# Joining the score and output products of neighbouring units on TensorE, in an mLSTM and two-layer MoE kernel

## The chip, the core and the metric

The kernel runs on one core of one Trainium2 chip. The metric is the device time of one execution in microseconds; smaller is better. Before the change three executions gave 732.37, 736.55 and 738.30 us, so the median is 736.55 us.

## What is computed

Three stages follow each other. The first is an mLSTM recurrence over 768 time steps, for 4 batches of 8 heads of width 40. The other two are feed-forward layers on the 3072 tokens that come out, each 320 wide.

```python
for t in range(S):                                   # first stage, per batch and head
    m_new = maximum(f_gate + m, i_gate)
    C = exp(f_gate + m - m_new) * C + exp(i_gate - m_new) * outer(v, k)
    n = exp(f_gate + m - m_new) * n + exp(i_gate - m_new) * k
    y[t] = sigmoid(o_gate) * (C @ q) / maximum(abs(n @ q), 1)
x = ((x @ w1) * (x @ w2) @ w3) @ w_out               # second stage, inner width 1024
y = maximum(maximum(x @ w1, x @ w2), x @ w3) @ w_out # third stage, inner width 768
```

The weights of the two feed-forward stages arrive as 64-bit floats, and the kernel turns them into 32-bit floats itself.

## The kernel before, in words

**The recurrence** is cut into 9 chunks per batch (8 of L = 88 steps and one of 64). A *unit* is one chunk of four heads; there are 72 units (`NU`), numbered u, two per chunk. `unit(u)` records the work of one: loads of q and k (`raw`, for the first ten units `raw0`), of keys and values (`kv`), of q once more (`qq`), of the gate row maxima (`dd`, from a small table `d_na` that the kernel itself writes to memory at the start); POOL and ACT turn `dd` into exponential weights; TensorE forms the scores `s` (L565 for the first ten units, L586 after them); DVE multiplies them by the weights into `pk` (L596); TensorE forms the outputs `o` from `pk` and `kv` (L606). In rows 88 to 127 `kv` holds the state that is carried from unit u to unit u + 2 (DVE, L611), so the chain from o to o goes on through the whole stage. DVE divides (L624 to L627), POOL multiplies by the output gate (L632) and pads (L636). When both units of a chunk are through, `x_cols` turns the chunk round on TensorE with three transposes (L646, called X here) and splits it into a high and a low part.

**The feed-forward stages** run over 8 blocks of 384 tokens. A product of 32-bit accuracy is made of several TensorE passes over the high and low parts. `group` (L678 to L682) makes one product of 8 matmuls of 384 columns; `b_step` (L745 to L749) and `d_step` (L764) make the second products. `fold` (L906) multiplies `w3` by `w_out` once, at the start. The weights come through `granule`: a load of 512 KB into one of four staging buffers (`stg`, `sx`), then about six ACT and DVE instructions that make 32-bit floats of it, then a split into parts (`wah` on ACT, `wal` on POOL or DVE, and so on).

**The order.** Every operation is recorded in a list with a duration, and `Plan.run` sets the order of each engine with these durations, the latencies between engines in `LAT`, one shift per kind of operation in `BIAS`, and a model of the transfers (`XFER`). Each engine then works through its own list in that order, and an instruction that has to wait holds up all behind it. All transfers are issued by SP, in one order too. `USTEPS` and `UNEXT` say behind which feed-forward steps a unit is recorded.

The buffers that matter: `s`, `o` and X share two PSUM banks (`aq`); `kv` has three buffers, `pk` two, `dd` four; the gate tiles of the start share memory with the `og` tiles of the output gate.

Of the kernel before, what the change touches and what calls it, by code (L numbers as in the profile page):

```python
# [17 lines left out]
L = 88  # L18
LP = 96
NCH = 9  # L20
# [8 lines left out]
NP = 10  # L29
FOLDS = (3,6,9)  # L30
# [10 lines left out]
RAW0 = 3  # L41
LAST = (NBLK - 1, 1, NC - 1)
# [3 lines left out]
    PA=200, PV=200, AV=130, AG=160, GA=90, GV=90, VA=130, VG=155, VP=200, AP=200, GP=230, DA=-50, DV=-50, DG=-30, DP=-50,  # L46
# [4 lines left out]
XFER = 1.45  # L51
BIAS = {"Add": -32750, "Aev": 31250, "Ag": -210500, "Akst": -383000, "Aph": -77500, "Aqs": -262250,
        "Asa": -13500, "Asg": 43250, "Astg": 57250, "Asx": 232000, "Awa": 7750, "Awar": -174000,
        "Awb": -221500, "Awc": 71000, "Awcr": -19750, "Awd": -55000, "Axh": -124000, "Dcs": -138250,
        "Ddd": 34000, "Ddna": 62500, "Dev": 75000, "Dg": -534000, "Dkv": 54250, "Dkvb": -129250, "Dqq": -96500,
        "Draw": 58250, "Dsg": -183000, "Dstg": 57750, "Dsx": -234500, "Dvs": 56750, "Gdd": 194250,
        "Gg": 144250, "Gmp": -23000, "Gpk": -77750, "Gpl": 36250, "Gqqb": -55750, "Gqs": -400500,
        "Gvsb": 10500, "Gwa": 379750, "Gwar": 219500, "Gwc": 102000, "Gwcr": 176500, "Gwd": 49000,
        "Gy": -128500, "Pac0": 27250, "Pac1": -309750, "Pac2": -91000, "Po": 7500, "Ppt": -14000, "Ps": -61250,
        "Pwk": 14250, "Pxt": -39750, "S-": -110000, "Sg": -305500, "Vam": -30000, "Vev": 474750, "Vg": -54250,  # L60
        "Vkst": 81500, "Vkv": -147750, "Vmp": -268500, "Vpk": -108500, "Vsa": -44000, "Vsg": 32250,
        "Vstg": 104500, "Vsx": -56500, "Vwb": -108500, "Vxl": 80250, "Vy": -35250, "Vzero": -14500}
# [5 lines left out]
USTEPS = (8, 9, 11, 12, 15, 16, 20, 21, 23, 25, 27)  # L68
# [209 lines left out]
def mlstm_moe_kernel(  # L278
# [45 lines left out]
    for pool_, tag, bufs, n in (  # L324
# [3 lines left out]
        (tmp, "sx", EX, 1024), (tmp, "w3", L_BUFS, 512), (tmp, "raw0", RAW0, 8 * L),  # L328
# [130 lines left out]
    for c in range(SIGN):  # L459
        dma(318, lambda c=c: SP.dma_start(out=sg0[0:LP, c], in_=og[0, c]), w=[("sg", (0, c))])  # L460
# [502 lines left out]
    def more():  # L963
        u = cur[0]
        if u < NU:
            unit(u)
            if u % 2:
                pend.append(ub(u)[:2])
# [156 lines left out]
```

## Time and profile before

| what | value |
|---|---|
| median of three executions | 736.55 us (732.37 to 738.30) |
| the profiled execution, its own time | 735.73 us |
| its span, from the first to the last instruction | 733.9 us |
| TensorE matmuls busy | 695.5 us (95%) |
| DVE, ACT, POOL busy | 453.4, 385.7, 337.2 us |
| mean granted TensorE clock | 0.988 of 2.4 GHz |

The profile is one execution. Of a row of the timeline the first number is the start, and the second is how long the instruction was in work. Matmuls overlap, so what a group of them costs is read from start to start: from the start of its first matmul to the start of whatever follows. A row of the windows view gives, for a stretch, how long each engine was busy, the granted clock, the mean busy share of the 16 DMA engines and the rate they moved.

### The profile page before, as it was taken

To read this page: it belongs to the slowest core of one execution; us is meant where nothing else is said; L and a number is where in the kernel's file an instruction comes from. 1 tells how busy PE (TensorE), PEld (TensorE's weight loads), DVE (VectorE), ACT (ScalarE), POOL (GpSimd) and SP (SyncE) were. 2 spreads that over 40 slices of the span, in tenths; PEclk is the share of its full clock that TensorE was granted. 3 is DMA by queue.
4 is the path that set the end of the run, shared out by engine and by line. 5 is a ranking of instruction groups with operands and counts; after the bars stand their busy time and mean duration, and the time that the engine had idled before them with its cause. 6 is when DMAs were issued, how large, how long until landed. Compare 5 with 4: busy or idle time off the path is not lost.

```text
span 733.9 us, 12690 instructions
## 1 busy us (share of the span) xinstructions
PE 695.5 (95%) x4269; PEld 670.2 (91%) x4269; DVE 453.4 (62%) x1012; ACT 385.7 (53%) x728; POOL 337.2 (46%) x465
## 2 busy tenths in 40 slices
PE   1797899999999999999999999999999999999998
PEld 1675887788999999999999999999999999999998
DVE  4679998878775668475454777564454774232433
ACT  5978989888884336545334345554342342232211
POOL 1859875857744345565423555564243461000000
PEclk9999999999999999999999999999999999999999
DMA  8998777955623335433212446332222340000000
GB/s 211 251 268 244 226 217 236 239 153 161 190 88 87 102 82 148 130 92 87 75 30 70 114 102 169 94 101 80 57 68 64 92 108 1 1 0 1 1 28 27
DMA packets 52232, 82.48 MB, mean 112 GB/s; under 512 B 11864, under 2 KB 37912, under 8 KB 52168
## 3 DMA queue, kind: packets, MB, share of 16 engines
q1 hardware_dynamic: 52168, 81.69, 40.3%
q8 instruction: 33, 0.54, 0.3%
q14 instruction: 31, 0.25, 0.1%
HBM read 77.63 MB, written 4.03 MB: 111 GB/s over the span
## 4 chain that ended last, share of the span: by engine, by line
PE 78%; DMA 7%; DVE 4%; ACT 4%; POOL 3%; issue 2%; SPq 0%; POOLq 0%; DVEq 0%; ACTq 0%
PE wk L678 12%; PE wk L680 12%; PE wk L679 12%; PE ac L764 8%; PE aq L606 6%; PE wk L682 6%; PE wk L681 6%; PE ac L745 4%; PE ac L749 4%; DMA dd<-d_na 4%; PE ac L747 3%; PE aq L586 2%; PE wk L906 1%; PE aq L646 1%; ACT stg L850 1%
## 5 line engine op out<-in xcount | busy, mean ns | idle before, releaser
L698 POOL TENSOR_TENSOR pl<-pr,ph 128x384 fp32r<-128x384 f32 (+1 forms) x30 | 31.2, 1040 | 161.1 <-ACT ph L694 141.9
L694 ACT CAST ph<-pr 128x384 fp32r<-128x384 f32 (+1 forms) x114 | 57.4, 507 | 86.3 <-PE ac L764 38.3
L678 PE MATMUL wk<-xh,wch 128*128 128x384 f32 x288 | 99.6, 346 | 0.2 <-ACT pr L726 0.2
L729 DVE TENSOR_TENSOR pr<-pr,wk 128x384 f32<-128x384 f32 (+1 forms) x98 | 53.2, 545 | 71.0 <-PE wk L682 67.9
L680 PE MATMUL wk<-xl,wch 128*128 128x384 f32 x288 | 97.1, 337 | 0.0
L679 PE MATMUL wk<-xh,wcl 128*128 128x384 f32 x288 | 97.0, 337 | 0.0
L698 DVE TENSOR_TENSOR pl<-pr,ph 128x384 fp32r<-128x384 f32 (+1 forms) x84 | 53.6, 638 | 67.3 <-ACT ph L694 66.5
L678 PE MATMUL wk<-xh,wah 128*128 128x384 f32 x256 | 91.7, 358 | 1.6 <-ACT xh L657 1.6
L680 PE MATMUL wk<-xl,wah 128*128 128x384 f32 x256 | 87.5, 342 | 2.8 <-DVE xl L660 2.8
L679 PE MATMUL wk<-xh,wal 128*128 128x384 f32 x256 | 87.4, 342 | 0.8 <-DVE wal L869 0.8
L575 POOL TENSOR_TENSOR qs<-misc,qs 40x352 fp32r<-40x352 f32 (+1 forms) x62 | 66.4, 1072 | 39.8 <-ACT qs L571 37.9
L541 POOL TENSOR_TENSOR dd<-am,dd 128x352 f32<-128x352 f32 (+2 forms) x72 | 59.9, 831 | 53.8 <-DMA dd<-d_na 49.1
L726 ACT COPY pr<-wk 128x384 f32<-128x384 f32 x48 | 23.2, 484 | 89.8 <-PE wk L682 89.8
L632 POOL TENSOR_TENSOR misc<-misc 88x160 f32<-88x160 f32 (+1 forms) x62 | 42.6, 687 | 54.5 <-DVE misc L627 54.2
L711 ACT COPY pr<-wk 128x384 f32<-128x384 f32 x64 | 31.0, 484 | 68.6 <-PE wk L682 68.6
L606 PEld LDWEIGHTS aq<-kv,pk 128*128 128x128 f32 (+2 forms) x496 | 59.3, 184 | 5.0 <-issue 2.2
L713 DVE TENSOR_TENSOR pr<-pr,wk 128x384 f32<-128x384 f32 x64 | 35.4, 553 | 41.7 <-PE wk L682 40.7
L606 PE MATMUL aq<-kv,pk 128*128 128x41 f32 (+2 forms) x496 | 58.9, 268 | 1.7 <-DVE misc L627 1.4
L850 ACT ACTIVATE stg<-stg 128x512 f16<-128x512 f32 (+2 forms) x41 | 52.2, 1281 | 7.4 <-DVE stg L842 6.7
L549 ACT ACTIVATE dd<-dd 128x352 f32<-128x352 f32 (+2 forms) x72 | 35.2, 490 | 39.9 <-POOL dd L545 36.0
L678 PEld LDWEIGHTS wk<-xh,wch 128*128 128x128 f32 x288 | 54.2, 188 | 0.5 <-ACT pr L726 0.5
L679 PEld LDWEIGHTS wk<-xh,wcl 128*128 128x128 f32 x288 | 54.2, 188 | 0.0
(130 smaller groups left out, 1755.7 us busy)
## 6 DMA issues: line engine op xcount, KB each, us to landing
misc<-in_qk SPq DMA_DIRECT2D x62, 330.0 KB
dd<-d_na SPq DMA_DIRECT2D x56, 176.0 KB
kv<-in_kv SPq DMA_DIRECT2D x72, 121.5 KB
stg<-in_w3t SPq DMA_DIRECT2D x13, 512.0 KB
stg<-in_wc SPq DMA_DIRECT2D x9, 512.0 KB
qq<-in_qk SPq DMA_DIRECT2D x64, 66.0 KB
misc<-in_og SPq DMA_DIRECT2D x31, 120.0 KB
out<-misc SPq DMA_DIRECT2D x23, 160.0 KB
```

Of the source, the lines that this page charges most:

```text
L541: P.op("G", 735, lambda: G.tensor_tensor(out=T("dd", u)[:r], in0=am[:r, c, h0:h0 + 4].unsqueeze(2).to_broadcast([r, 4, n]), in1=T("dd", u) ...
L575: P.op("G", 889, lambda: G.tensor_tensor(out=T("qs", u)[0:40], in0=T("raw", u)[0:40, 0, :, 0:n], in1=T("qs", u)[0:40].bitcast(F32), op=ALU ...
L606: PE.matmul(T("o", u)[:m, h], lhsT=T("pk", u)[:r, h, 0:m], rhs=T("kv", u)[:r, h, 40:81], start=True, stop=True)
L678: PE.matmul(p, lhsT=h_[:, kt], rhs=xh[:, kt], start=kt == 0, stop=False)
L679: PE.matmul(p, lhsT=l_[:, kt], rhs=xh[:, kt], start=False, stop=False)
L680: PE.matmul(p, lhsT=h_[:, kt], rhs=xl[:, kt], start=False, stop=False)
L681: PE.matmul(p, lhsT=r_, rhs=xh[:, 2], start=False, stop=False)
L694: P.op("A", act(n), lambda sl=sl: A.copy(out=T("ph", key)[:, sl], in_=T(*src)[:, sl]), r=[src + part], w=[("ph", key) + part])
L698: e.tensor_tensor(out=T("pl", key)[:, sl], in0=T(*src)[:, sl], in1=T("ph", key)[:, sl].bitcast(F32), op=ALU.subtract)
L729: P.op("V", dve(sl.stop - sl.start), lambda ps=ps, sl=sl: V.tensor_tensor(out=T(*sc)[:, sl], in0=T(*sc)[:, sl], in1=T(*ps)[:, sl], op=ALU. ...
L764: PE.matmul(T(f"ac{m}", (k, 1)), lhsT=src[:, m * 128:m * 128 + 128], rhs=w[:, o:o + DM], start=first_, stop=last_,)
L850: A.activation(out=sign, in_=tl()[:, :, 1].bitcast(F32), func=AF.Copy)
```

## The change

- From unit `DUO` = 28 on, the matmuls of s(u) and of o(u - 1) are recorded as one TensorE operation, s first. The rest of unit u - 1 (state, division, gate) and the loads of unit u + 2 are recorded behind it.
- The loads of `kv` and of the output gate have 88 rows and no longer 96; those of `qq` and of `raw0` have 40 and no longer 48. A row of `raw0` is cut into four pieces of 704 bytes.
- In `raw0` there is room for an identity behind k, which ACT writes three times at the start. No unit uses it, since `Q0` lists units 2 to 17.
- `LAT`, `BIAS`, `XFER`, the durations of the transfers and `USTEPS` (one more unit step) have new values, so all engines have a new order.

```diff
-LP = 96
+Q0 = tuple(range(2, 18))
+DUO = 28
 LAT = dict(
-    PA=200, PV=200, AV=130, AG=160, GA=90, GV=90, VA=130, VG=155, VP=200, AP=200, GP=230, ...
+    PA=200, PV=200, AV=165, AG=210, GA=90, GV=90, VA=130, VG=155, VP=200, AP=200, GP=230, ...
-XFER = 1.45
+XFER = 1.5
-BIAS = {"Add": -32750, "Aev": 31250, "Ag": -210500, ...
+BIAS = {"Add": -98000, "Aev": 80000, "Ag": -244500, ...
-USTEPS = (8, 9, 11, 12, 15, 16, 20, 21, 23, 25, 27)
+USTEPS = (8, 9, 11, 12, 15, 16, 20, 21, 23, 25, 26, 27)
...
+    eye = cs[0:40, 0:40].unsqueeze(1).to_broadcast([40, 4, 40])
+    for i, t in enumerate(slots["raw0"]):
+        P.op("A", act(160), lambda t=t: A.copy(out=view(t, [40, 4, 128 + L], F32)[:, :, 2 * L:128 + L], in_=eye),
+             r=[("cs", 0)], w=[("raw0b", i)])
...
-        dma(322, lambda: SP.dma_start(out=T("kv", u)[0:LP], in_=kv[b, g, c]), w=[("kv", u, "k")])
+        dma(317, lambda: SP.dma_start(out=T("kv", u)[0:L], in_=kv[b, g, c]), w=[("kv", u, "k")])
...
-            new(t, [LP, DM], F32, "og")
-            dma(318, lambda x=x, t=t: SP.dma_start(out=T(*t), in_=og[b, x]), w=[t])
+            new(t, [L, DM], F32, "og")
+            dma(313, lambda x=x, t=t: SP.dma_start(out=T(*t), in_=og[b, x]), w=[t])
...
-            new(("raw", u), [48, 4, 2 * L], F32, "raw0")
-            dma(333, lambda: SP.dma_start(out=T("raw", u), in_=qk0[g, c]), w=[("raw", u)])
+            new(("raw", u), [40, 4, L + 128], F32, "raw0")
+            dma(313, lambda: SP.dma_start(out=T("raw", u)[:, :, 0:2 * L], in_=qk0[g, c]), w=[("raw", u)])
...
-            dma(174, lambda: SP.dma_start(out=T("qq", u)[80:128], in_=qk[b, g, c, 56:104, 0]),
+            dma(157, lambda: SP.dma_start(out=T("qq", u)[L:128], in_=qk[b, g, c, 0:40, 0]),
...
+            duo = u >= DUO
+            if duo:
+                new(("o", u - 1), [128, 4, 41], F32, "aq")
             def f():
                 for h in range(4):
                     PE.matmul(T("s", u)[0:L, h], lhsT=ks[:, h], rhs=T("qs", u)[:, h], start=True, stop=True)
-            P.op("P", 390, f, cols=90, r=[("qs", u), ("kst", u % 2)], w=[("s", u)])
+                if duo:
+                    outs(u - 1)
+            if duo:
+                P.op("P", 1210, f, cols=300, r=[("qs", u), ("kst", u % 2), ("pk", u - 1), ("kv", u - 1)],
+                     w=[("s", u), ("o", u - 1)])
+            else:
+                P.op("P", 390, f, cols=90, r=[("qs", u), ("kst", u % 2)], w=[("s", u)])
...
+        if u >= DUO:
+            rest(u - 1)
+            load(u + 2)
+        if u + 1 < DUO or u == NU - 1:
+            new(("o", u), [128, 4, 41], F32, f"ac{u % 3}" if u < 10 else "aq")
+            P.op("P", 910 if m > n else 500, lambda: outs(u), cols=210, r=[("pk", u), ("kv", u)], w=[("o", u)])
+            rest(u)
+
+    def outs(u):
+        b, c, g, n, r = ub(u)
+        m = 128 if c < NCH - 1 else n
+        for h in range(4):
+            PE.matmul(T("o", u)[:m, h], lhsT=T("pk", u)[:r, h, 0:m], rhs=T("kv", u)[:r, h, 40:81], start=True, stop=True)
```

**TensorE.** No matmul is added or taken away; only the order is another. On TensorE at the X of the 24th chunk, before (`qs` and `kst` are q and k of s, here of unit 48; the matmuls from `cs` and `misc` are X):

```order
L681 MATMUL wk_129<-xh_81,war 128x384
L682 MATMUL wk_129<-xl_84,war 128x384
L586 MATMUL aq_132<-qs_94,kst_74 88x88 x4
L646 MATMUL aq_133<-cs,misc 128x88 x3
L678 MATMUL wk_130<-xh_81,wah 128x384
```

Before, X stands right behind the s of a later unit, and o stands alone; the whole program has 28 such pairs of s and X, and 6 pairs of s and o. On TensorE a little further on, at s of unit 56 and o of unit 55, now:

```order
L773 MATMUL ac_135<-pl_88,wb 128x384
L598 MATMUL aq_132<-qs_94,kst_74 88x88 x4
L629 MATMUL aq_133<-kv_104,pk_97 128x41 x4
L702 MATMUL wk_130<-xh_81,wah 128x384
L703 MATMUL wk_130<-xh_81,wal 128x384
```

Now o follows s directly, in 46 pairs, and 25 of the 36 X stand alone between large products (before 3); 6 still follow an s. Of the last 24 chunks, 21 had two large products between the o that completes the chunk and its X, and three had three; now there are three or more for 23 of them, and two for the last.

**SP, the first loads.** On SP, behind the gate loads at the start, before (`sx0`, `stg0`, `stg1` are staging buffers, `in_wo1` and `in_w3t` weights):

```order
L488 DMA kv1_104<-in_kv 96x324
L437 DMA d_na_76<-misc_137 8x9x88
L526 DMA raw00_126<-in_qk0 48x704
L828 DMA stg0_111<-in_wo1 128x1024
L502 DMA misc_137<-in_og 96x320 x4
L535 DMA dd0_90<-d_na_76 88x352
L535 DMA dd1_91<-d_na_76 88x352
L828 DMA sx0_121<-in_wo1 128x1024
```

On SP at the same place now:

```order
L494 DMA kv2_105<-in_kv 88x324
L508 DMA misc_137<-in_og 88x320 x4
L852 DMA stg0_111<-in_wo1 128x1024
L439 DMA d_na_76<-misc_137 8x9x88
L852 DMA stg1_112<-in_wo1 128x1024
L852 DMA sx0_121<-in_wo1 128x1024
L543 DMA dd0_90<-d_na_76 88x352
L543 DMA dd1_91<-d_na_76 88x352
L543 DMA dd2_92<-d_na_76 128x352
L543 DMA dd3_93<-d_na_76 128x352
L852 DMA stg0_111<-in_w3t 128x1024
L533 DMA raw00_126<-in_qk0 40x4x176
```

The write of `d_na`, the first `dd` and the first `raw` moved behind the gate tiles and three to four weight loads: by the shapes, 4.07 MB are issued up to and with the first `dd` (before 3.18 MB).

**ACT and DVE.** Ahead of the first product's evacuation ACT now has 91 instructions (before 83) and DVE 124 (before 118), since weight decoding moved forward and three `wal` and three `war` parts moved from POOL to DVE. Ahead of the eleventh it is 193 against 191 on ACT and 247 against 249 on DVE.

## Rows read from the trace of the kernel before

**Rows 1.** Windows: stretch, us; busy us of PE, PEld, DVE, ACT, POOL; clock; DMA; GB/s

```profile
20.00:60.00 40.00, 35.62 (x175) 29.73 (x176) 29.58 (x74) 33.35 (x48) 28.90 (x44) 0.96 0.95 268
60.00:200.00 140.00, 128.10 (x728) 115.88 (x727) 120.53 (x242) 123.92 (x218) 104.30 (x122) 0.95 0.71 203
200.00:640.00 440.00, 438.63 (x2816) 432.06 (x2816) 262.35 (x623) 194.18 (x401) 196.35 (x281) 1.00 0.33 87
```

**Rows 2.** Chain that ended last, first 25 us: start us, us, what

```profile
12.65 5.58 DMA dd<-d_na
...
22.95 1.93 PE ac L606 x8
```

**Rows 3.** Timeline of SP, first 13 us: start us, us, the issues

```profile
9.55 0.29 SPq L437 DMA_DIRECT2D d_na<-misc  x1
...
10.77 1.79 SPq L502 DMA_DIRECT2D misc<-in_og  x4
```

**Rows 4.** Timeline of PE: an s alone, then an o alone

```profile
303.90 0.44 PE L586 MATMUL aq<-qs,kst 120*88 120x88 f32 x4
304.17 0.42 PE L678 MATMUL wk<-xh,wah 128*128 128x384 f32 x1
304.43 0.34 PE L679 MATMUL wk<-xh,wal 128*128 128x384 f32 x1
...
309.23 0.98 PE L606 MATMUL aq<-kv,pk 88*128 88x41 f32 x8
310.04 0.42 PE L678 MATMUL wk<-xh,wah 128*128 128x384 f32 x1
```

**Rows 5.** Timeline of PE: s, with o behind it (78.87), and the next product

```profile
78.60 0.44 PE L586 MATMUL aq<-qs,kst 120*88 120x88 f32 x4
...
79.76 0.42 PE L678 MATMUL wk<-xh,wah 128*128 128x384 f32 x1
```

**Rows 6.** Timeline of PE: X beside s, first, a held and last case

```profile
190.82 0.39 PE L646 MATMUL aq<-cs,misc 88*128 88x88 f32 x3
191.00 0.49 PE L586 MATMUL aq<-qs,kst 120*88 120x88 f32 x4
...
224.35 0.44 PE L586 MATMUL aq<-qs,kst 120*88 120x88 f32 x4
...
224.85 0.42 PE L678 MATMUL wk<-xh,wch 128*128 128x384 f32 x1
...
316.67 0.48 PE L586 MATMUL aq<-qs,kst 120*88 120x88 f32 x4
...
317.43 0.59 PE L646 MATMUL aq<-cs,misc 88*128 88x88 f32 x2 [0.15 <-POOL misc L632]
317.81 0.42 PE L678 MATMUL wk<-xh,wah 128*128 128x384 f32 x1
...
608.55 0.43 PE L586 MATMUL aq<-qs,kst 120*88 120x64 f32 x4
...
609.06 0.42 PE L678 MATMUL wk<-xh,wah 128*128 128x384 f32 x1
```

**Rows 7.** Transfers: packets by size; issues by line, count, KB each

```profile
DMA packets 52232, 82.48 MB, mean 112 GB/s; under 512 B 11864, under 2 KB 37912, under 8 KB 52168
...
misc<-in_qk SPq DMA_DIRECT2D x62, 330.0 KB
...
kv<-in_kv SPq DMA_DIRECT2D x72, 121.5 KB
...
qq<-in_qk SPq DMA_DIRECT2D x64, 66.0 KB
misc<-in_og SPq DMA_DIRECT2D x31, 120.0 KB
...
raw<-in_qk SPq DMA_DIRECT2D x10, 132.0 KB
...
vs<-in_vs SPq DMA_DIRECT2D x64, 15.4 KB
```

More of the change, by code (lines that the diff above doesn't have):

```diff
@@ L327, in mlstm_moe_kernel @@
         (big, "kv", BUF["kv"], 324), (big, "vs", BUF["vs"], 164), (big, "qq", BUF["qq"], 4 * L), (big, "stg", STG, 1024), (big, "pr", NPR, TB),
-        (tmp, "sx", EX, 1024), (tmp, "w3", L_BUFS, 512), (tmp, "raw0", RAW0, 8 * L),
+        (tmp, "sx", EX, 1024), (tmp, "w3", L_BUFS, 512), (tmp, "raw0", RAW0, 4 * (128 + L)),
         (psum, "wk", 3, 512), (psum, "aq", 2, 512), *((psum, f"ac{i}", 1, 512) for i in range(3)),
@@ L459, in mlstm_moe_kernel @@
     for c in range(SIGN):
-        dma(318, lambda c=c: SP.dma_start(out=sg0[0:LP, c], in_=og[0, c]), w=[("sg", (0, c))])
+        dma(313, lambda c=c: SP.dma_start(out=sg0[0:L, c], in_=og[0, c]), w=[("sg", (0, c))])
         sig.append(P.op("A", 360 + (1283 if c == 0 else 0), lambda c=c: A.activation(
-            out=sg0[0:LP, c], in_=sg0[0:LP, c], func=AF.Sigmoid
+            out=sg0[0:L, c], in_=sg0[0:L, c], func=AF.Sigmoid
         ), w=[("sg", (0, c))]))
@@ L520, in unit @@
     def unit(u):
-        load(u + 2)
+        if u < DUO:
+            load(u + 2)
         b, c, g, n, r = ub(u)
@@ L564, in f @@
                 for h in range(4):
-                    PE.matmul(T("s", u)[:L, h], lhsT=raw[0:40, h, L:2 * L], rhs=raw[0:40, h, 0:n], start=True, stop=True)
-            P.op("P", 720, f, r=[("raw", u)], w=[("s", u)])
+                    PE.matmul(T("s", u)[:rs, h], lhsT=raw[:, h, L:L + rs], rhs=raw[:, h, 0:n], start=True, stop=True)
+            P.op("P", 870 if rs == 128 else 640, f, r=[("raw", u), ("raw0b", u % RAW0)], w=[("s", u)])
         else:
@@ L596, in unit, with rest @@
         P.op("V", dve(4 * n), lambda: V.tensor_tensor(
-            out=T("pk", u)[:L, :, 0:n], in0=T("s", u)[:L], in1=T("dd", u)[:L], op=ALU.mult
+            out=T("pk", u)[:rs, :, 0:n], in0=T("s", u)[:rs], in1=T("dd", u)[:rs], op=ALU.mult
         ), r=[("s", u), ("dd", u)], w=[("pk", u, 1)])
-        if u < 10:
-            new(("o", u), [128, 4, 41], F32, f"ac{u % 3}")
-        else:
-            new(("o", u), [128, 4, 41], F32, "aq")
-        def f():
-            for h in range(4):
-                PE.matmul(T("o", u)[:m, h], lhsT=T("pk", u)[:r, h, 0:m], rhs=T("kv", u)[:r, h, 40:81],
-                          start=True, stop=True)
-        P.op("P", 910 if m > n else 500, f, cols=210, r=[("pk", u), ("kv", u)], w=[("o", u)])
-        if m > n:
+        if u >= DUO:
+            rest(u - 1)
+            load(u + 2)
+        if u + 1 < DUO or u == NU - 1:
[7 more added lines that the diff above has]
+            PE.matmul(T("o", u)[:m, h], lhsT=T("pk", u)[:r, h, 0:m], rhs=T("kv", u)[:r, h, 40:81], start=True, stop=True)
+    def rest(u):
+        b, c, g, n, r = ub(u)
+        if c < NCH - 1:
             P.op("V", dve(164), lambda: V.scalar_tensor_tensor(
@@ L637, in unit @@
                  r=[("y", (b, c), 1)], w=[("y", (b, c), 2)])
+            pend.append((b, c))
     def x_cols(b, c):
@@ L826, in tl @@
             return T(*key)[:, 0:n]
-        dma(n * 2.484, lambda: SP.dma_start(out=tl().rearrange("p a b -> p (a b)"), in_=src.bitcast(I32)),
+        dma(n * 2.844, lambda: SP.dma_start(out=tl().rearrange("p a b -> p (a b)"), in_=src.bitcast(I32)),
             w=[key])
@@ L1068, in _lay @@
         kvt[:, :, c, 0:n, :, 40:80] = vv[:, :, c * L:c * L + n]
[L1069 removed]
+    og = np.zeros((B, NCH, L, DM), f)
     oo = i["o_gate"].transpose(0, 2, 1, 3).reshape(B, S, DM)
```

45 lines of the change are left out of this document (21 added, 24 removed).

## The prediction

> **What bounds the kernel now.** I read the windows first. From 200 to 640 us TensorE is busy for 438.6 of 440 us at full clock, ACT and DVE for about half, and the DMA engines for a third [rows 1]. In that stretch only TensorE's own list counts: what its instructions cost in sequence, and the few holes in it. From 60 to 200 us TensorE is idle for 140 - 128.1 = 11.9 us at a granted clock of 0.95, while ACT works for 124 and DVE for 121 of 140 us; from 20 to 60 us the DMA engines are busy for 95% of the time at 268 GB/s and ACT for 33 of 40 us [rows 1]. So the start is held by transfers first, then by ACT and DVE together, and a better TensorE list alone gains nothing there. The chain of waits says the same: a `dd` transfer that is issued at 12.65 us and needs 5.58 us leads to the first o at 22.95 us [rows 2]. I cost the change in these two stretches apart, against the profiled execution (735.7 us, 0.8 below the median of the runs shown).
>
> **The join.** An s alone costs 0.27 us from its start to the next product's start (303.90 to 304.17), and then the next product's first matmul takes 0.26 us and not the usual 0.17 (304.17 to 304.43), so 0.36 in all. An o alone costs 0.81 us (309.23 to 310.04), with the same tail 0.90 [rows 4]. Apart they cost 1.26 us. s with o right behind it took 1.16 us from 78.60 to 79.76, with the tail 1.25 [rows 5]. So one tail of 0.09 us is saved, and 0.08 us of it is given back, because the weights of a lone o are loaded under the long matmul ahead of it, and behind the short matmuls of s they are not. There are 40 new pairs (46 against 6): 40 x 0.01 = 0.4 us. The change itself counts 0.09 us a pair (1210 for 390 + 910), which would be 3.6 us. I take the row, which is this very sequence on the chip: **0**, with 3.6 us of gain as the other end. On the loss side a join can hold s back until the previous unit's `pk` is there. The nearest joined units have two large products between them, 2.8 us, and DVE needs half a microsecond for `pk`. I cost that at nothing. If DVE is late, the 0.3 to 0.6 us that a held X costs now (next part) is the price of each case.
>
> **X away from s.** X right behind s takes 0.50 us with it where nothing holds it (224.35 to 224.85, and 608.55 to 609.06, the first and the last of 23 such groups between 200 and 640 us) [rows 6], 0.59 with the tail. X ahead of an s takes 0.18 us (190.82 to 191.00) [rows 6], so alone 0.27 with its tail, and s and X apart 0.63. About 22 pairs are split: 22 x 0.04 = **0.9 us lost**.
>
> **The wait of X.** The same groups show the only holes of size in this stretch. The one at 316.67 us took 1.14 us, since X waited for POOL's gating, L632 (317.43) [rows 6]. The 23 groups took 15.9 us together, against 23 x 0.50 = 11.5: 4.4 us of waiting. X stood two products and one s behind the o that completes its chunk, 3.05 us, and was ready up to 0.7 us later. Now three products or more stand between, 4.1 us, in all but one of the last 24 chunks. That covers it, with 0.3 us over; the multiply of the joined s also falls on DVE ahead of the division or behind it, and a few cases may still wait. I take **4.0 of the 4.4 us gained**; ends 2 and 4.4. What is late next is nothing that the profile shows between 200 and 640 us: the holes of all kinds there are 440 - 438.6 = 1.4 us beside the stretched X.
>
> **The shorter transfers.** The 72 `kv` loads go from 121.5 KB to 111.4, the gate's from 120 to 110, `qq` from 66 to 55, `raw0` from 132 to 110 [rows 7]. Up to unit 9 that is about 500 KB less, 1.9 us at 268 GB/s. But the packets say that this is not the whole cost. There are 11864 packets under 512 bytes [rows 7]; 4864 of them are data (the small pieces of `dd` in the last chunks, of `d_na` and of the identity), so 7000 are completions. The transfers of that view number 463, and 16 completions each would be 7408. The 408 that are missing are what one finds if a transfer runs on the largest number of engines up to 16 that divides its rows: 15 for the 62 loads of 120 rows (62 missing), 12 for the 64 `vs` loads of 24 rows (256 missing) [rows 7], and 90 for three small kinds, 408 to the piece. By that count 96 and 48 rows run on 16 engines, 88 on 11, and 40 on 10. Then one engine of those used carries 10.1 KB of a `kv` load and not 7.6, 10.0 and not 7.5 of a gate tile, 5.5 and not 4.1 of `qq`, 11.0 and not 8.25 of `raw0`. At 268 GB/s over 16 engines that are 95% busy an engine moves 17.6 KB a microsecond, so units 0 to 9 (10 `kv`, 9 gate, 8 `qq`, 10 `raw0`) load the busiest engines with 4.9 us more, in the stretch where they are full. The Trainium skill ("DMA: Bandwidth & Descriptors", "Why a DMA increments its semaphore by 16 and not by 1") states this rule, and that it is the lowest-numbered engines that are used; the count of completions agrees with the first part, and nothing here shows the second.
>
> **The new order of the start.** The write of `d_na` moves behind the gate tiles. It was issued at 9.55 us, and four gate issues take 1.79 us, from 10.77 us on [rows 3]; with one weight load behind them `d_na` goes out at about 12.9 us, the first `dd` as much later, and 0.89 MB more stand ahead of it (3.3 us at 268 GB/s). So the first o comes at 26 to 27 us and not at 22.95. It is not lost time as such: weights are decoded meanwhile. Ahead of the first product ACT has 8 and DVE 6 instructions more, ahead of the eleventh 2 more and 2 fewer: the loan is paid back by about 150 us. In a stretch that ACT and DVE bound, equal work ahead of equal products gives equal time. I take **0** for the start as a whole; ends: 4.9 us of DMA and some 4 us of late o lost on one side, half of the 11.9 us of holes gained on the other.
>
> Sum: 735.7 - 0.4 + 0.9 - 4.0 + 0 = **732.2 us**, and the median stands 0.8 above this execution: **732.5**. The last products keep their distance from the last results, so the end is as before.
>
> **The rivals.**
> - *The start gets longer* (0.25). Its place is the first 70 us, its price the 4.9 us of the busiest engines, and, where unit 9 thereby comes late enough, the 4 us of the first o too: 737 to 741 us, slower than before. It decides if the first large product starts more than 4 us later and ACT and DVE have no slack left to catch up. For it: 95% busy, and the count of completions. Against it: ACT and DVE are idle for 16 and 19 of the 140 us after 60 [rows 1], which is room to catch up. The rule of the Trainium skill named above speaks against the change here; by whole rows on 16 engines the shorter loads would give 1.9 us.
> - *The start gets shorter* (0.15). The longer latencies take holes out of the order there too. Half of the 11.9 us: about 726 us. For it: X is held in the same way before 200 us. Against it: ACT and DVE are near their limit, so a hole that closes in one place opens in another.
> - *The waits only move* (0.10). The join puts o's chain a few microseconds later, and what X saves is lost ahead of the joined s: 735 to 737 us.
>
> The forecast itself has 0.5. The range takes in the shorter start and the longer one: 725 to 742 us. About 1%, 7.4 us, is what a measurement of this kernel can tell from no change. Faster than that, below 729.2 us, are nearly all of the shorter start and a fifth of the forecast: 0.24. Slower, above 743.9 us, needs both losses of the start and no gain of X: 0.11. The rest is 0.65.
>
> **What would show it.** In the changed kernel's timeline X should go through in 0.18 us in nearly all chunks after 200 us, and the idle time that L632 and L636 end on TensorE should all but vanish. A joined pair should take 1.16 us to the next product, not 1.07. The packets under 512 bytes should fall by 72 x 5 for `kv`, 36 x 5 for the gate tiles, 64 x 6 for `qq` and 10 x 6 for `raw0` completions, 984 in all. The first o should come at 26 to 27 us, and TensorE should have done as much by 150 us as before. I am wrong if the stretch from 200 to 640 us is not shorter for the same work, or if TensorE is more than 3 us behind or ahead at 200 us.

## The result, and the profile after

The changed kernel takes 745.2 us (median of four runs, 738.6 to 746.3) against 737.0 us: a ratio of 1.010, 95% interval 1.006 to 1.014. It is **slower by 8 us**; I had forecast 732.5 us, with a range up to 742. Its profiled execution, the longest of the four, spans 744.5 us, 10.6 more than the one shown before the change.

The windows of the changed kernel, in the columns of [rows 1] (busy us and count of each engine, granted clock, DMA share, GB/s):

```profile
20.00:60.00 40.00, 30.60 (x127) 22.51 (x128) 21.66 (x52) 28.59 (x39) 20.02 (x29) 0.77 0.67 207
60.00:200.00 140.00, 127.47 (x728) 112.40 (x728) 116.96 (x245) 119.42 (x206) 100.32 (x122) 0.93 0.69 195
200.00:640.00 440.00, 436.39 (x2812) 430.91 (x2811) 278.97 (x641) 204.73 (x422) 202.58 (x285) 1.00 0.33 90
```

From 20 to 60 us every engine is now idle for longer than before the change. ACT falls from 33 to 29 us of 40, DVE from 30 to 22, POOL (the last busy column) from 29 to 20, and the DMA share from 0.95 to 0.67. Nothing is full, and yet less is done. The engines wait for each other. (The clock column has no record from before TensorE's first rise and counts that time as full; more on this below.)

TensorE's timeline, start and duration, with the idle time before it and its releaser in brackets, shows where the time is. First the start, answering to [rows 2]: first s, first o, two groups of the fold, the last X ahead of the first large product, and that product.

```profile
26.27 1.47 PE L573 MATMUL aq<-raw 40*88 40x88 f32 x8 [15.89 <-DMA raw<-in_qk]
29.02 1.90 PE L629 MATMUL ac<-kv,pk 88*128 88x41 f32 x8 [1.27 <-DVE pk L614]
...
46.06 4.63 PE L930 MATMUL wk<-wof,w 128*128 128x320 f32 x8 [1.06 <-DVE w L880]
...
53.21 4.63 PE L930 MATMUL wk<-wof,w 128*128 128x320 f32 x8
57.77 1.47 PE L573 MATMUL aq<-raw 40*88 40x88 f32 x8
59.17 1.93 PE L629 MATMUL ac<-kv,pk 128*128 128x41 f32 x8
...
72.51 0.85 PE L573 MATMUL aq<-raw 40*88 40x88 f32 x8
...
83.89 0.89 PE L670 MATMUL aq<-cs,misc 88*128 88x88 f32 x2 [3.23 <-POOL misc L655]
...
86.14 0.67 PE L702 MATMUL wk<-xh,wah 128*128 128x384 f32 x1
```

The first o comes at 29.0 us (22.95 before), the first large product at 86.1 us. Before the change it came at 69.0:

```profile
69.02 0.44 PE L678 MATMUL wk<-xh,wah 128*128 128x384 f32 x1 [1.60 <-ACT xh L657]
```

It starts 17 us later. Some of that is caught up: counting each product at its price at full clock (an estimate, from the starts of products that follow each other), TensorE has done 135.9 us of its work by 200 us, 144.7 before, so it is 8.8 us behind. Another 3.7 us go between 200 and 240 us, in holes such as this one, where s waits for DVE:

```profile
200.58 0.34 PE L706 MATMUL wk<-xl,wcr 128*128 128x384 f32 x1
202.17 0.51 PE L598 MATMUL aq<-qs,kst 120*88 120x88 f32 x4 [1.25 <-DVE misc L650]
```

Behind 260 us there are next to no holes in either kernel, and the changed one needs 1.6 us less for its shorter list (fewer changes between small and large products). 8.8 + 3.7 - 1.6 = 10.9 us; the two profiled executions end their last product 10.6 us apart.

The order of the transfers on SP, answering to [rows 3] (start and duration of the issues):

```profile
9.98 1.48 SPq L508 DMA_DIRECT2D misc<-in_og  x4
11.51 0.36 SPq L852 DMA_DIRECT2D stg<-in_wo  x1
11.97 0.29 SPq L439 DMA_DIRECT2D d_na<-misc  x1
12.31 0.35 SPq L852 DMA_DIRECT2D stg<-in_wo  x1
13.69 0.35 SPq L852 DMA_DIRECT2D sx<-in_wo  x1
17.26 1.58 SPq L543 DMA_DIRECT2D dd<-d_na  x4
19.81 0.33 SPq L852 DMA_DIRECT2D stg<-in_w3t  x1
20.18 0.79 SPq L533 DMA_DIRECT2D raw<-in_qk  x1
```

`d_na` goes out at 11.97 us, behind gates and one weight piece, and the first `dd` at 17.26 us, 4.6 us later than before. `raw` of unit 0 comes behind four weight pieces. In the chain of waits the first o of 29.0 us follows a weight piece's work on DVE (L880, 27.37 to 28.43 us), which stands there ahead of the `pk` that the o needs.

What this does to POOL is the plainest sight of all. These are POOL's waits, whole time, number and longest, before the change up to 70 us:

```profile
POOL dd L541 <- DMA dd<-d_na: 18.9, 6, 12.7
...
POOL pk L555 <- PE ac L606: 0.2, 1, 0.2
```

and in the changed kernel up to 90 us:

```profile
POOL dd L549 <- DMA dd<-d_na: 16.1, 1, 16.1
POOL pk L610 <- PE aq L670: 9.4, 1, 9.4
POOL pk L563 <- PE ac L629: 8.5, 2, 6.2
```

Before, POOL waited for TensorE for 0.2 us in all. Now it waits 17.9 us. POOL's timeline shows the longest case and how the queue behind it stands:

```profile
51.77 0.50 POOL L553 TENSOR_SCALAR_AFFINE_SELECT dd<-dd 88x352 f32<-88x352 f32 x1
61.68 0.94 POOL L610 TENSOR_TENSOR pk<-qq,dd 64x352 f32<-64x352 f32 x1 [9.41 <-PE aq L670]
62.69 0.46 POOL L563 TENSOR_TENSOR pk<-kv,dd 128x160 f32<-128x160 f32 x1
```

From 52.3 to 61.7 us POOL stands at one multiplication that, by the profile, waits for what TensorE does at 59 to 61 us, and two groups of the fold at 4.6 us each lie ahead of that on TensorE. The chain of waits runs on TensorE up to 63.2 us and from there mostly on POOL, up to the X of 83.9 us.

The granted clock is 0.5, the lower of TensorE's two levels, from 42.0 to 65.9 us and from 76.1 to 89.8 us, 37.5 us in all; before it was 17.1 us in four short pieces. But the record starts at the first rise, at 35.1 us here and at 45.9 us before, and by the lengths of the products TensorE was at the lower level until then: an s of four products takes 1.47 us at 26.27 us, and before the change 1.45 at 38.69 and 0.85 at 46.34. With that time the lower level lasted some 73 us here and 63 before, so the two kernels differ in it by 10 us and not by 20.

The steady part answers to [rows 4 to 6]. An X that is held, an X ahead of a large product, and a joined pair:

```profile
278.55 0.68 PE L670 MATMUL aq<-cs,misc 88*128 88x88 f32 x2
279.44 0.29 PE L670 MATMUL aq<-cs,misc 88*128 88x88 f32 x1 [0.21 <-POOL misc L659]
...
291.81 0.39 PE L670 MATMUL aq<-cs,misc 88*128 88x88 f32 x3
291.99 0.42 PE L702 MATMUL wk<-xh,wah 128*128 128x384 f32 x1
...
305.77 0.44 PE L598 MATMUL aq<-qs,kst 120*88 120x88 f32 x4
306.04 1.06 PE L629 MATMUL aq<-kv,pk 88*128 88x41 f32 x8
306.93 0.78 PE L769 MATMUL ac<-ph,wb 128*128 128x384 f32 x3
```

The pair takes 1.16 us (305.77 to 306.93) and X 0.18 us (291.81 to 291.99), both as forecast; X does so in 17 of the 20 chunks of 88 rows between 240 and 640 us. The packets, answering to [rows 7]:

```profile
DMA packets 50993, 80.43 MB, mean 108 GB/s; under 512 B 10880, under 2 KB 37152, under 8 KB 50928
```

Those under 512 bytes fell from 11864 to 10880, by 984, the number that the count of engines gave.

### The profile page after: what moved, and what is told of

Its sections match the earlier page's. It is cut to its first block, busy times and chain, and to the rows that moved or that the text cites. A ratio compares the mean times of both kernels' runs of the same rounds, so it can differ in the third digit from the quotient of the medians.

```text
span 744.5 us, 12591 instructions
## 1 busy us (share of the span) xinstructions
PE 696.8 (94%) x4269; PEld 667.8 (90%) x4269; DVE 461.5 (62%) x1015; ACT 389.9 (52%) x738; POOL 329.0 (44%) x453
## 2 busy tenths in 40 slices
DMA packets 50993, 80.43 MB, mean 108 GB/s; under 512 B 10880, under 2 KB 37152, under 8 KB 50928
## 4 chain that ended last, share of the span: by engine, by line
PE 76%; POOL 6%; ACT 5%; DVE 5%; DMA 3%; issue 3%; SPq 1%; POOLq 0%; DVEq 0%; ACTq 0%
PE wk L702 12%; PE wk L703 11%; PE wk L704 11%; PE ac L788 8%; PE aq L629 6%; PE wk L706 5%; PE wk L705 5%; PE ac L769 4%; PE ac L773 3%; PE wk L930 3%; PE ac L771 2%; PE aq L598 2%; DMA stg<-in_wo 2%; ACT stg L874 2%; PE ac L629 1%
## 5 line engine op out<-in xcount | busy, mean ns | idle before, releaser
L722 DVE TENSOR_TENSOR pl<-pr,ph 128x384 fp32r<-128x384 f32 (+1 forms) x87 | 59.7, 687 | 78.5 <-ACT ph L718 76.9
L722 POOL TENSOR_TENSOR pl<-pr,ph 128x384 fp32r<-128x384 f32 (+1 forms) x27 | 28.8, 1068 | 150.3 <-ACT ph L718 128.6
L583 POOL TENSOR_TENSOR qs<-misc,qs 40x352 fp32r<-40x352 f32 (+1 forms) x62 | 63.0, 1018 | 22.8 <-ACT qs L579 22.5
L750 ACT COPY pr<-wk 128x384 f32<-128x384 f32 x48 | 22.9, 478 | 83.5 <-PE wk L706 83.4
L629 PE MATMUL aq<-kv,pk 128*128 128x41 f32 (+2 forms) x496 | 62.1, 275 | 0.8 <-DVE xl L684 0.5
L563 POOL TENSOR_TENSOR pk<-kv,dd 128x160 f32<-128x160 f32 (+1 forms) x64 | 35.9, 562 | 56.0 <-PE aq L629 41.8
L629 PEld LDWEIGHTS aq<-kv,pk 128*128 128x128 f32 (+2 forms) x496 | 57.5, 184 | 3.4 <-DVE xl L684 1.2
```

The costliest lines, as they stand in the source:

```text
L583: P.op("G", 889, lambda: G.tensor_tensor(out=T("qs", u)[0:40], in0=T("raw", u)[0:40, 0, :, 0:n], in1=T("qs", u)[0:40].bitcast(F32), op=ALU ...
L629: PE.matmul(T("o", u)[:m, h], lhsT=T("pk", u)[:r, h, 0:m], rhs=T("kv", u)[:r, h, 40:81], start=True, stop=True)
L722: e.tensor_tensor(out=T("pl", key)[:, sl], in0=T(*src)[:, sl], in1=T("ph", key)[:, sl].bitcast(F32), op=ALU.subtract)
```

## The experiments

Ratios are to the kernel before, measured on the same chip, with 95% intervals. "FLP" is the start of the first large product (69.0 us before, 86.1 in the changed kernel), each from one profiled execution; e1_join_off, whose order is the changed kernel's up to there, has 84.5, so a difference of 1.6 us between two FLPs means nothing. Experiments ran on different chips, so two of them are best compared by their ratios.

**The rows of the transfers.** In the changed kernel, with its plan and every engine's order kept:

```diff
-        dma(317, lambda: SP.dma_start(out=T("kv", u)[0:L], in_=kv[b, g, c]), w=[("kv", u, "k")])
+        dma(317, lambda: SP.dma_start(out=T("kv", u)[0:LP], in_=kv[b, g, c]), w=[("kv", u, "k")])   # LP = 96; og, qq, raw0 likewise
```

> The changed kernel, its plan and the order of every engine kept, but the transfers carry 96 and 48 rows again (unused rows added to gates, keys, scaled queries and raw0). Rows theory (88 rows on 11 engines and 40 on 10 cost up to 4.9 us at the start): 739 to 742 us, first s before 26 us, first large product at 81 to 84 us. Order theory (the loads come in a worse order, whatever their rows) and clock theory (TensorE at half clock): no change, 743 to 747 us, first large product within 1.5 us of 86.

745.4 us, 1.010 (1.006 to 1.014), FLP 85.6 us. The rows theory falls. The counterpart gives the real rows to the kernel before, whose order on all engines stays row for row:

> The kernel before with the transfers' real rows of 88 and 40 and nothing else: every engine runs the order of the kernel before. Prediction's sum for this part: up to 4.9 us on the busiest DMA engines by unit 9, paid back later, so 736 to 741 us. If the rows cost nothing (as e1_rows96 says): ratio 0.997 to 1.003, and the first o at 21.6 us as in e1_start_undone.

736.9 us, 1.001 (0.999 to 1.003), first o at 23.1 us, FLP 70.2. Its window from 20 to 60 us shows why it costs nothing:

```profile
20.00:60.00 40.00, 34.81 (x172) 29.10 (x173) 28.96 (x72) 31.97 (x46) 28.10 (x42) 0.96 0.84 250
```

The mean busy share of the 16 DMA engines went from 0.95 to 0.84 and the bytes per second from 268 to 250, while TensorE, DVE, ACT and POOL did nearly the same. Those 95% were not the limit that I took them for.

**The start's order undone.** Up to unit 28 the planner uses the biases, latencies and estimates of the kernel before, and the three copies of the identity are left out:

```diff
-        self.bias.append(BIAS.get(eng[0] + (w or r or ("-",))[0][0], 0))
+        tab = BIAS0 if self.early else BIAS          # early: recorded before unit 28; BIAS0: table of the kernel before
+        self.bias.append(tab.get(eng[0] + (w or r or ("-",))[0][0], 0))
```

(latencies, transfer factor and estimates in the same way.)

> The changed kernel with the order of the kernel before on every engine up to unit 28 (its biases, latencies and estimates for all work recorded before unit 28, and without the three copies of eye); real rows of 88 and 40, the join and the new tables from unit 28 on. Order theory: the 55 us that TensorE lost by 180 us fall back to about 46 and the join still gives its 3 to 4 us: 731 to 736 us, first large product at 66 to 70 us. Rows theory: 739 to 742. Join theory (the joined order itself costs 8 us or more): 742 to 747.

734.0 us, 0.997 (0.995 to 0.9995), FLP 69.8 us: the order theory holds. All that the change loses lies in what was undone. The copies of the identity are not needed for a loss: e3_first_loads_late and the two e6 kernels below lack them too and lose by their order alone. TensorE's first steps there:

```profile
12.32 1.47 PE L588 MATMUL aq<-raw 40*88 40x88 f32 x8 [1.94 <-DMA raw<-in_qk]
21.65 1.93 PE L644 MATMUL ac<-kv,pk 88*128 88x41 f32 x8 [7.86 <-POOL pk L578]
```

**Join and tables, apart.** Four kernels make a square with the start of the kernel before and real rows: old tables or, behind unit 28, the new ones, without and with the join (`DUO = 100` and `DUO = 28`, the latter with the one more unit step). Two corners are e2_rows_alone (neither) and e1_start_undone (both); these are the others.

> As e2_rows_alone, and the join from unit 28 on, with the tables of the kernel before throughout. If the join takes X's waits away (prediction): 3 to 4 us below e2_rows_alone. If the tables do it (from 240 to 640 us TensorE's small products cost 66.3 us before, 62.2 in e1_start_undone, 64.2 in e1_join_off without a join): within 1 us of e2_rows_alone, the small products at 65 to 67 us.

> As e1_start_undone without the join: tables of the kernel before up to unit 28, the new ones behind it. If the tables take X's waits away: 1.5 to 3 us below e2_rows_alone, equal to e1_start_undone within 1 us. If the join does: equal to e2_rows_alone within 1 us.

The join alone: 735.4 us, 0.999 (0.997 to 1.002). The tables alone: 732.8 us, 0.9965 (0.995 to 0.998). The small products between 240 and 640 us, worked out from the starts of TensorE's products and brought to equal numbers of s and o, cost 63.7 us with neither, 63.2 with the join, 62.2 with the tables and 62.2 with both. So the join takes half a microsecond off TensorE's list at most. It does take X's waits away, and so do the tables. The table counts, for the same stretch, what X of 88 rows took above its shortest case (0.50 us behind an s, 0.18 alone) and what the joined pairs took above 1.16 us:

| | X's waits | the joined pairs' waits |
|---|---|---|
| neither | 3.1 | 0.0 |
| the join | 1.0 | 1.7 |
| the tables | 1.4 | 0.0 |
| both | 0.8 | 1.0 |

The join moves most of the waits from X to the joined pairs. (The kernel before, whose order is that of the first row, has 4.0 and 0.2, so a difference of 1 us is not much.) The same with the changed kernel's own start:

```diff
-DUO = 28
+DUO = 100
-USTEPS = (8, 9, 11, 12, 15, 16, 20, 21, 23, 25, 26, 27)
+USTEPS = (8, 9, 11, 12, 15, 16, 20, 21, 23, 25, 27)
```

> The changed kernel without the join (its start, up to about 240 us, is the same on every engine; eleven units a round as before). Prediction's own sum: the join takes 3 to 4 us of waits away, so without it 747 to 750 us. Join theory (the joined order costs): 737 to 742 us.

741.0 us, 1.007 (1.005 to 1.009), FLP 84.5 us: in the range of the join theory, and 4 us below the changed kernel's median, or 2 by the ratios, whose intervals overlap. Not all of it is the join's: of the 3.5 us by which the last product of this profile comes earlier, 1.6 are there at the first large product, where both kernels have the same order. In the square the join costs 1.2 us with the new tables (734.0 against 732.8) and gains 1.5 with the old ones (735.4 against 736.9), neither beyond the intervals. So a gain of 3 to 4 us shows nowhere; whether the join costs something in the changed kernel stays open.

**The clock.** 127 products of zeros go into TensorE's idle places, all other work in the same order:

```diff
+                    if e == "P":
+                        for _ in range(FILL.get(pos[0], 0)):       # FILL = {1: 44, 2: 4, 4: 10, ..., 32: 20}: before TensorE's n-th step
+                            order.append((t, -1, lambda s=s: self.fill(s)))
```

> The changed kernel with 127 products of zeros (128x384, no result used) put into TensorE's own idle places between 9 and 86 us; the order of all other work on every engine is kept. Clock theory (TensorE works at half clock from 42 to 66 and 76 to 90 us, and from 30 us to 74 us it is hardly ever idle): granted clock 1.0 through most of 15 to 90 us, first large product at 74 to 79 us, 735 to 739 us. Order theory in its form that the data come late: the clock rises too, but first large product at 83 to 88 us and 742 to 746 us.

747.5 us, 1.016 (1.013 to 1.020), FLP 88.5 us. The windows (columns as above) of this kernel, and then of the changed one:

```profile
45.00:55.00 10.00, 9.42 (x40) 7.32 (x40) 7.96 (x18) 4.50 (x9) 7.99 (x13) 0.66 0.64 195
55.00:70.00 15.00, 14.81 (x102) 12.52 (x100) 9.68 (x23) 10.77 (x16) 7.66 (x10) 0.98 0.58 163
```

```profile
45.00:55.00 10.00, 8.94 (x29) 6.15 (x29) 5.94 (x12) 5.28 (x9) 6.59 (x10) 0.50 0.68 208
55.00:70.00 15.00, 15.00 (x75) 11.80 (x73) 8.68 (x22) 10.08 (x15) 7.83 (x10) 0.64 0.54 144
```

The clock rose from 0.64 to 0.98 between 55 and 70 us, and POOL still began its chain at 62.0 us (61.7). The last 20 zero products, which took 5.0 us, stood in the way, which I misjudged: X was through at 83.5 us, so without them the first large product would have come at some 85 us. But this does not price the clock, since earlier zeros stood in the way too:

```profile
57.52 2.14 PE L481 MATMUL wk<-zero 128*128 128x384 f32 x10
59.59 0.85 PE L580 MATMUL aq<-raw 40*88 40x88 f32 x8
```

TensorE was busy for 26.8 of the 27 us from 47 to 74 us of this run, and from 51.8 to 59.6 us zeros took 4.4 us of it, directly ahead of s products; whether those could have started earlier isn't shown. So the run shows that this way of raising the clock doesn't help, and no more. Two later experiments bound what the clock does (short fold and relief, below).

**Fold later.** In the changed kernel the six groups of the fold wait for the s of later units (`after=[zs[...]]`), and the planner orders the rest anew.

> The changed kernel, but the six groups of the fold may come on TensorE only behind the s of units 6, 8, 8, 9, 9 and 9 (the planner orders the rest anew by the changed kernel's tables). Fold theory (in the changed kernel the fold's 8 products of 0.53 us each stand on TensorE ahead of units 1 to 9, and the chain of the units, with its work on POOL, starts late): first large product at 68 to 76 us and 734 to 739 us. If only the first loads matter (gates and weights ahead of d_na and raw: first s at 26 us instead of 12): first large product still at 80 us or later, 741 to 746 us.

743.5 us, 1.010 (1.008 to 1.012), FLP 81.3 us: the numbers of the second expectation, but not its reason, for the first s came at 15.3 us and not at 26. The first o came at 28.8 us all the same, and of the fold's last groups, which now stood right ahead of the first large product, two took 7.1 us at the lower clock. Since the planner moved everything else too, this tells little.

**The first transfers alone, both ways.** Only SP's issues from the third key tile on are exchanged, 21 in the changed kernel and 18 in e1_start_undone; the other engines keep their order.

```diff
-        kv og og og og wo d_na wo wo dd dd dd dd w3t raw wo w3t raw raw w3t dd      # the changed kernel
+        d_na raw wo og og og og dd dd wo dd dd kv wo raw raw w3t wo w3t w3t dd      # e3_first_loads_back
```

> The changed kernel, of which only the order of 21 transfers on SP is other (from the third key tile to the fifth dd): d_na first, then raw of unit 0, a weight piece, the four gate tiles, dd of units 0 to 3 with one weight piece between, as the kernel before has them. TensorE, VectorE, ScalarE and GpSimd keep the changed kernel's order row for row. First-loads theory (gates and weights ahead of d_na and raw make first s 14 us and first o 6 us late, and the whole start with them): first s at 13 to 16 us, first o at 22 to 25 us, first large product at 72 to 80 us, 735 to 740 us. Order theory (what stands late is the order on the compute engines, the fold's groups ahead of the units): first o at 22 to 25 us too, but first large product at 82 us or later, 742 to 746 us.

> The counterpart: e1_start_undone (734.0 us), of which only the order of 18 transfers on SP is that of the changed kernel: the third key tile, the four gate tiles and a weight piece ahead of d_na, two more ahead of the dd, raw behind them. All other engines as in e1_start_undone. First-loads theory: first o at 28 to 29 us, first large product at 76 to 82 us, 740 to 745 us. Order theory: the 6 us are caught up, first large product at 70 to 73 us, 733 to 737 us.

Back: 744.2 us, 1.010 (1.007 to 1.013), FLP 86.3. Late: 739.1 us, 1.003 (1.001 to 1.006), FLP 74.3. So the late loads cost 4 to 5 us in the old order of the engines (739.1 - 734.0; 0.6% by the ratios), between the two expectations, and moving them back brings nothing clear of the noise in the new one (1.010 both), as the order theory said. Its first o, forecast at 22 to 25 us, came at 30.1. ScalarE's timeline in e3_first_loads_back shows why:

```profile
22.46 0.70 ACT L888 ACTIVATE stg<-stg 128x512 f32<-128x512 f32 x1 [3.78 <-DMA stg<-in_wo]
23.20 1.33 ACT L905 ACTIVATE stg<-stg 128x512 f16<-128x512 f32 x1
24.55 1.28 ACT L588 ACT_TABLE_LOAD   x1
25.84 0.88 ACT L588 ACTIVATE dd<-dd 88x352 f32<-88x352 f32 x2
```

The `dd` are there early, but ScalarE has the weight pieces ahead of the exponentials in its order and now waits for those. TensorE's first o is then no earlier, although its first s is:

```profile
12.70 1.47 PE L604 MATMUL aq<-raw 40*88 40x88 f32 x8 [2.34 <-DMA raw<-in_qk]
30.14 1.90 PE L660 MATMUL ac<-kv,pk 88*128 88x41 f32 x8 [15.97 <-issue]
```

**Short fold and relief of GpSimd.** For the two fold kernels, which leave out three of every four products of the first three folds, the changed one and e1_start_undone with

```diff
-                for i in range(4):
-                    gt = q * 4 + i
+                for i in range(1 if ft < 3 else 4):
+                    gt = q * (7 if ft < 3 else 4) + i
```

and for the relief `order.append((t, j, ops[j][2][1 if j in self.relief else a]))`, which gives the scaled products of units 2 to 9 to VectorE at their place.

> The changed kernel with one product of four in each of the first six groups of the fold (the first three folds are left incomplete); the order on every engine is kept. On TensorE 20.9 us of fold before the first large product become some 5. Fold theory: first large product at 70 to 76 us, 730 to 736 us, and the distance to e4_short_fold_undone falls from 11 to under 5 us. If GpSimd's chain holds the start: first large product at 80 us or later, 740 to 744 us, the distance stays over 8 us.

> e1_start_undone with the same six groups cut to one product of four. Its fold takes some 15 us of TensorE before 69 us, between waits for transfers. Both theories: 727 to 733 us, first large product at 62 to 69 us; what counts is its distance to e4_short_fold_after.

> The changed kernel with the four scaled products of units 2 to 9 that the plan put on GpSimd in the start (0.93 us each) moved to VectorE at the same place of the order; all else kept. GpSimd theory (the chain of waits runs on GpSimd from 62 to 86 us, three of these products in it): first large product at 82 to 84.5 us, 741 to 743.5 us. If GpSimd only follows: first large product within 1 us of 86 and 744 to 747 us.

Short fold: 740.4 us, 1.004 (1.001 to 1.007), FLP 81.6; undone 733.9 us, 0.9945 (0.991 to 0.998), FLP 68.7. The distance falls from 11 to 6.5 us, between the two expectations. In both of these kernels TensorE is at its lower level all the way to the first large product (the first rise comes at 85.7 and 76.2 us). So here is a comparison at equal clock and with a quarter of the fold, and the FLPs still lie 12.9 us apart, against 16.3 with the whole fold (86.1 and 69.8): neither the clock nor the length of the fold is the main part of the late start.

Relief: 741.9 us, 1.007 (1.004 to 1.010), FLP 80.8, the time that the GpSimd theory gave, though its interval overlaps the changed kernel's. POOL's time at TensorE's door fell to 2.3 us, but waits for ACT and others took its place:

```profile
...
POOL pk L564 <- issue: 5.5, 1, 5.5
POOL pk L564 <- ACT wb L940: 4.4, 1, 4.4
POOL pk L564 <- PE ac L632: 2.3, 1, 2.3
```

But the 5.4 us by which the first large product is earlier are not what POOL no longer does after 62 us. They are there before: the o that comes at 61.37 us in the changed kernel comes at 55.73 here. One piece is the clock, which was at its upper level from 49.7 to 56.5 us of this execution, so that the fold's group of 53.21 us in the changed kernel (4.63 us) took half as long:

```profile
50.80 2.42 PE L933 MATMUL wk<-wof,w 128*128 128x320 f32 x8
```

So the clock can move the first large product by a few microseconds. Executions of one kernel differ in the same way: in e1_rows96 the one with the highest mean granted clock (0.986) took 739.3 us and the one with the lowest (0.974) 746.4.

The next two take the cures together: first loads and relief, then the short fold as well.

> The changed kernel with the first transfers in the order of e3_first_loads_back and the four scaled products on VectorE as in e4_pool_relief. If the parts add up: 1.1 and 3.4 us below the changed kernel, 740 to 742 us. If the first loads only count once GpSimd is free (they are 5 us in the order of the kernel before, e3_first_loads_late): 735 to 739 us. If they cover each other: 741 to 744 us.

> The same with the six groups of the first three folds cut to one product of four (three folds are left incomplete). If the three parts are the whole of the start's loss: 732 to 736 us, level with e4_short_fold_undone (733.9), first large product at 68 to 73 us. If something else in the order holds it: 737 us or more, first large product at 76 us or later.

746.1 us, 1.014 (1.009 to 1.019), and 745.2 us, 1.012 (1.007 to 1.017), FLP 83.5 and 85.2. The first, from four executions of 741.8 to 749.0 us, is beyond every expectation, the second (three executions) says that something else holds the start: together the cures give nothing that these few executions show. In e5_all_three the clock is part of it:

```profile
71.13 1.47 PE L605 MATMUL aq<-raw 40*88 40x88 f32 x8
```

With less fold on TensorE, an s of four products takes 1.47 us at 71 us, where the changed kernel needs 0.85 (at 72.51): TensorE, with less to do, is still at the lower of its two levels (the first rise comes at 89.9 us). So the short fold did not only take work away, and its time alone can't be used as the measure that I meant it to be.

**How far into the start.** The whole order of one engine can't be exchanged alone between the two starts: the engines would wait for one another for good. A piece of time on all five engines can. In e1_start_undone the work of the first 30 and of the first 62 us of the plan is sorted into the changed kernel's order:

```diff
+            own = [i for i, x in enumerate(q) if x[1][1] in RANK]       # RANK: place in the changed kernel's order
+            new_ = sorted((q[i][1] for i in own), key=lambda x: RANK[x[1]])
```

> e1_start_undone (734.0 us), in which the work that the plan starts in its first 30 us is put, on all five engines, into the changed kernel's order: gate tiles and weight pieces ahead of d_na and raw, two weight pieces ahead of the first exponentials on ScalarE; the fold's groups stay where the kernel before has them. If the loss is made in these first 30 us: 741 to 745 us, first large product at 80 us or later. If it is made behind: as e3_first_loads_late, 737 to 740 us, first large product at 72 to 76 us.

> The same with the work of the first 62 us: TensorE, VectorE and SP have the changed kernel's order up to the first large product, with the fold's groups between the units; behind it the order of e1_start_undone. If the start alone makes the changed kernel slow: 742 to 746 us, first large product at 82 to 88 us. If what stands behind the first product is needed too (the 3 to 4 us lost at 200 to 240 us in the changed kernel): 738 to 741 us.

| the changed kernel's order in | time | ratio | FLP |
|---|---|---|---|
| nothing (e1_start_undone) | 734.0 | 0.997 (0.995 to 0.9995) | 69.8 |
| the first 18 transfers (e3_first_loads_late) | 739.1 | 1.003 (1.001 to 1.006) | 74.3 |
| the first 30 us, all engines | 741.9 | 1.006 (1.004 to 1.008) | 78.6 |
| the first 62 us, all engines | 749.5 | 1.0165 (1.013 to 1.020) | 84.3 |
| the changed kernel | 745.2 | 1.010 (1.006 to 1.014) | 86.1 |

The loss grows step by step. With the first 30 us 7 to 8 us are lost, while the fold's groups are where the kernel before had them; the order of the next 32 us, with the fold between the units, adds as much again. The start alone is worse than the whole changed kernel; that the changed kernel's later order fits this start better is likely, but not shown.

**A version that beats both.** e2_tables_alone with 43 products of zeros in TensorE's two idle places at 11 and 13 to 22 us:

> e2_tables_alone (732.8 us) with 43 products of zeros in TensorE's two idle places at 11 and 13 to 22 us, the order of all other work kept. If half the clock costs at the start (the chain of waits of e2_rows_alone runs on TensorE from 23.1 to 30.7 us, at half clock): first key transfer of the chain 3 us earlier, first large product at 66 to 68 us, 729 to 731 us. If the loads set the start: first large product at 69 to 71 us, 732 to 734 us.

731.6 us, 0.9936 (0.991 to 0.996), FLP 68.7 us, beside 0.9965 without them. Both beat the kernel before and the changed one. Whether the zeros add anything is open: the intervals overlap, and the clock fell again at 25.8 us.

## Why the prediction was wrong

**The sum.** It has two slips: it subtracts 0.4 us for the join, for which 0 was taken, and 732.2 and 0.8 make 733.0, not 732.5. Neither matters beside 745.2.

**The join: right in the main.** 0 was taken; TensorE's list gained half a microsecond at most, the whole time moved by -1.5 and +1.2 us in the square, and the pair takes the 1.16 us of [rows 5]. The holding of joined units was put at nothing: 5 of 39 pairs took 1.22 to 1.47 us in the changed kernel, 0.9 us together.

**X away from s and its waits: right on X, too large in all.** X goes through in 0.18 us in nearly all chunks, as forecast. Its waits between 240 and 640 us, above its shortest cases, fell from 4.0 to 1.6 us, by 2.4 and not by 4 (of the 4.4 us that I counted, 0.4 are two chunks of 64 rows, whose X takes longer without a wait). The mechanism, that the join takes X away from the o it waits for, is borne out by the join alone (3.1 to 1.0 us in the square). But the tables do it without the join (1.4), and with the join most of the waits turn up again at the joined pairs, as the rival "The waits only move" had it. And I had left out that there would be new holes between 200 and 240 us: they cost 3.7 us (0.8 with the start undone, by the same count), so from 200 to 640 us the changed kernel is some 2 us slower for the same work, where the sum had it 3.5 us faster.

**The shorter transfers: the count right, the price wrong.** The Trainium skill's rule ("DMA: Bandwidth & Descriptors", "Why a DMA increments its semaphore by 16 and not by 1"), the largest divisor up to 16, gives the 984 packets to the piece. But the 4.9 us on the busiest engines do not show: 1.001 (0.999 to 1.003) for the rows alone.

**The new order of the start: this step failed.** It read: "In a stretch that ACT and DVE bound, equal work ahead of equal products gives equal time. I take 0", and that the loan "is paid back by about 150 us". The first half of the sentence was false. ACT and DVE were busy for 124 and 121 of 140 us [rows 1], and I took a busy engine for a full one. The start is bound by the order: each unit's chain goes from a transfer over POOL, ACT, TensorE and DVE back to the next unit, and each engine takes its work in the order written. Put weight pieces and the fold ahead of it and the engines have the same work, but stand idle in front of it: POOL for 17.9 us at TensorE, where it had been 0.2. The loan was 17 us and not 4, some 11 of it were still owed at 150 us, and 8.8 at 200. At equal clock and with a quarter of the fold it would still have been 12.9 (the two short folds). I had costed the late `d_na` at 3 to 4 us for the first o (26 to 27 us forecast, 29.0 measured) and left out of the sum what stood behind it: `raw` of unit 0 behind four weight pieces, ScalarE's pieces ahead of the exponentials, the fold ahead of the units on TensorE. All were to be read from the order of the changed kernel beforehand.

**The rivals.** "The start gets longer" was the right place, and its condition was met (the first large product over 4 us later). Its mechanism, the busiest DMA engines, was not the one, so its 737 to 741 us were too low. Both of my marks for being wrong were met: TensorE was over 3 us behind at 200 us, and the stretch from 200 to 640 us was not shorter for the same work.

What stays open: which engine's place in the new start order costs most, and how much of the loss goes through the clock. The mixtures of single engines' orders that would tell can't be run, since the engines would wait for one another for good, and the cures overlap.

## What to carry to other kernels

Busy shares do not show that a stretch is bound by an engine: where a chain runs over five engines that each keep a written order, moving other work ahead of it can cost the wait, not the work. When a change moves the start, follow the first unit's chain through every engine's order, down to the first product of the main loop, and price each thing that now stands ahead of it. And measure tables and mechanism apart: here the tables that came with the join were worth more than the join, and their start cost more than both.

## What had not been expected of the hardware

- Transfers of 88 and 40 rows, on 11 and 10 engines by the count of completions, were no slower for the kernel than those of 96 and 48 on 16, in a stretch with the DMA share at 0.95 (736.9 against 735.7 us, 1.001).
- Work taken from TensorE can make its other products slower: with the first three folds cut to a quarter, the s of 71 us in e5_all_three took 1.47 us and not 0.85.
- The granted clock of a window can read full while TensorE is at its lower level: from 20 to 40 us the record shows 1.00 in the kernel before, and an s took 1.44 to 1.47 us there; after the first rise, at 46.34 us, 0.85.
- A load whose rows are cut into four pieces takes longer to issue: a `raw` took SP 0.78 to 0.81 us in e2_rows_alone and 0.31 to 0.41 in the kernel before, again at no cost to the kernel.
